# Attention chunk states from two running products, four pairs transposed on chip, and the whole instruction order in a table

## The chip, the cores and the metric

The kernel runs on one core of one Trainium2 chip. The metric is the device time of one execution in microseconds (us), lower is better. Engines: PE (matrix multiply), DVE (VectorE), ACT (ScalarE), POOL (GpSimd), and SP, whose queue issues every DMA.

## The reference, cut to what matters

A linear attention with a per-channel decay `w` is followed by two gated layers on the 3072 tokens.

```python
B, H, S, D = 4, 8, 768, 48
for t in range(S):                         # state: (B, H, D, D)
    cur = einsum('bhd,bhe->bhde', u[None] * k[:, :, t], v[:, :, t])
    y[:, :, t] = einsum('bhd,bhde->bhe', r[:, :, t], state + cur)
    state = w[:, :, t][..., None] * state + einsum('bhd,bhe->bhde', k[:, :, t], v[:, :, t])
x = y.transpose(0, 2, 1, 3).reshape(3072, 384)
x = ((x @ w_a) * (x @ w_b)) @ w_out                  # 384 -> 1536 -> 384
out = square(maximum(x @ w_in, 0)) @ w_out2          # 384 -> 2048 -> 384
```

## The kernel before

**Attention.** The sequence is cut into chunks of 64 tokens. Two chunks make a pair, and there are 24 pairs (6 for each of the 4 batches). All 8 heads of a pair are worked on together, with the even chunk on partitions 64 to 111 (`EV`) and the odd one on 0 to 47 (`OD`). For each pair, DVE forms the running product of the decays with one scan (`at_scan`, L307, into `ef`) and its reciprocals in four pieces of 128 columns (`at_recip`, L312). `k` times the reciprocal (`at_kr`, L316) and `r` times the product (`at_rr1` or `at_rr`) make all decays inside a chunk a product of two factors. `at_u1`, `at_u2` and `at_diag` form the diagonal term r·u·k from a second, untransposed copy of r and k (`nat`, 384 KB a pair). On PE a pair is four groups: A (scores, L361 and L362), B (transposes of k, L372), C (what each chunk adds to the state, L384 and L386) and D (outputs, L405 and L406). DVE merges the scores under a mask (L367, A2), and carries the state through both chunks with four operations (`at_C2`, L393 to L397). ACT copies D's result out of PSUM in two halves; SP stores it to `xd` in DRAM.

**Layers.** Weights arrive as 64-bit words, and each unit of layer weights is decoded by seven operations on ACT, DVE and POOL (L248, L252, L257 and L266 are those on DVE; L266 is the last). Every product is taken as three passes over high and low parts, so a block of n tokens costs 27 matmuls of n columns for each of the 12 units of the first layer (L431 to L433 up, L461 to L463 down) and 18 for each of the 16 of the second. The blocks of the first layer are `BLOCKS1 = [384, 256, 384] + [512] * 4`, so the first block needs pairs 0 to 2. Its tokens come back from `xd` (`plan_x`), are split into `xh` on ACT and `xl` on DVE (L631) or POOL, and the first matmul of the layer waits for the last `xl`.

**Order.** `Plan` orders all operations on all engines by costs and due times (`KNOB`), and every engine works through its own list in that order. For the first part of the program a table, `LEAD`, overrides the planner: each entry is an operation's number and, where it can run on several engines, a letter for the engine.

Of the kernel before, what the change touches and what calls it, by code (L numbers as in the profile page):

```python
# [27 lines left out]
BLOCKS1 = [384, 256, 384] + [512] * 4  # L28
# [6 lines left out]
EN = HE + HC  # L35
WS = 256.0

KNOB = dict(RC=42.49, START=12.8, LEAD=15.73, DEC=3.63, XO=5.02, X2=16.11, D2=32.51, LW=5.1, LT=30.17, LV=9.31,
            LV2=-10.85, LN=16.64, scan=3.63, rec=-5.73, kr=108.97, rr=-10.63, u1=0.34, u2=-43.62, dg=-15.47,
            gd=-190.45, UB=-979.54, A=9.27, B=166.95, C=-4.55, D=102.51, T2=4.07, EARLY=3.1, WAIT=0, U0=-2.33,  # L40
            DA=3.18, OB=26.94, P0=-44.22, P1=-28.21, P2=-11.48, P3=-11.11, P4=13.86, P5=83.07, P6=89.76, P7=90.37)
ENG = dict(kr=("POOL",), da=("DVE", "POOL"), dl=("DVE", "POOL"), rr=("POOL", "DVE"), u2=("DVE",), xs=("DVE",), d2=("ACT",),
           b2=("ACT",), gl=("POOL",), gh=("ACT",), dg=("POOL",), u1=("POOL",), ds=("DVE",))
ENG0 = dict(ENG, kr=("DVE",), rr=("POOL",))
NP0 = 7
ALONE = 8
SAFE = 2.0 ** 90
# [128 lines left out]
def fused_kernel(ctx, tc, tpk, natpk, vpk, v2pk, upk, cst, w1pk, w2pk, out):  # L176
# [126 lines left out]
    def inv(p):  # L303
        return EF[p][:, HE:]
# [644 lines left out]
```

## Time and profile before

| | |
|---|---|
| runs | 984.85, 987.32, 987.61 us, median 987.32 |
| the profiled execution | 984.9 us |
| its span, first to last instruction | 983.1 us |
| PE busy | 935.7 us, 95% of the span |
| DVE, ACT, POOL busy | 505.2, 387.6, 384.0 us |

The span is what the trace covers; the execution's own time is 1.8 us longer. A busy share of the whole says little here: the program starts with some 60 us of attention on four pairs and of decoding, in which PE is mostly idle, and then runs matmuls to its end. So the stretches are read one by one.

### The profile page before, as it was taken

The numbers are of one execution on the slowest core, as the hardware profiler recorded it, in microseconds if no ns is written. First come the engines' busy times: TensorE is split into PE (matmuls) and PEld (weight loads), VectorE is DVE, ScalarE is ACT, GpSimd is POOL, SyncE is SP. The second block draws the span as 40 slices with busy tenths as digits, with TensorE's granted clock in tenths as the row PEclk, the third lists the DMA queues.
The fourth block names the chain that finished last, engine by engine and source line by source line (L and its number), as shares of the span: only waits on it lengthen the run. The fifth ranks groups of instructions, "written<-read, shape, count | busy, mean of one in ns | idle before, by whom it ended". The sixth has DMA issues, their size and how long they took to land.

```text
span 983.1 us, 15022 instructions
## 1 busy us (share of the span) xinstructions
PE 935.7 (95%) x5982; PEld 799.3 (81%) x5982; DVE 505.2 (51%) x652; ACT 387.6 (39%) x600; POOL 384.0 (39%) x295
## 2 busy tenths in 40 slices
PE   2469999999999999999999999999999999999997
PEld 2459989999888888888888888888888888888885
DVE  7999999999755455532211789621121211211211
ACT  2677743343223332323322676433333333333332
POOL 5533177820165556543122444333333333333332
PEclk9569999999999999999999999999999999999999
DMA  8997336555022432220103562010000100100001
GB/s 224 258 288 225 112 89 178 145 162 157 25 82 81 139 108 69 85 65 29 48 33 113 193 212 95 0 65 1 33 33 1 53 11 1 65 1 1 33 0 36
DMA packets 58031, 87.17 MB, mean 89 GB/s; under 512 B 23904, under 2 KB 34912, under 8 KB 57952
## 3 DMA queue, kind: packets, MB, share of 16 engines
q1 hardware_dynamic: 57952, 86.12, 28.8%
q8 instruction: 49, 0.80, 0.3%
q14 instruction: 30, 0.25, 0.1%
HBM read 71.95 MB, written 14.16 MB: 88 GB/s over the span
## 4 chain that ended last, share of the span: by engine, by line
PE 84%; DVE 6%; DMA 6%; issue 1%; SPq 1%; ACT 0%; DVEq 0%; ACTq 0%
PE pa L431 15%; PE pa L432 15%; PE pa L433 15%; PE acc L461 11%; PE acc L462 11%; PE acc L463 11%; DMA raw<-in_w1pk_dram 2%; PE sc L361 2%; PE yp L405 2%; DMA rk<-in_tpk_dram 2%; DMA xd<-ys 1%; DVE ef L312 1%; DVE z L252 1%; PE ds L386 1%; DVE w L266 1%
## 5 line engine op out<-in xcount | busy, mean ns | idle before, releaser
L454 POOL TENSOR_TENSOR gl<-a,gh 128x512 fp32r<-128x512 f32 (+2 forms) x158 | 209.2, 1324 | 468.2 <-ACT gh L230 465.5
L431 PE MATMUL pa<-xh,w 128*128 128x512 f32 (+2 forms) x792 | 296.0, 374 | 1.4 <-ACT a L438 0.6
L432 PE MATMUL pa<-xl,w 128*128 128x512 f32 (+2 forms) x792 | 293.6, 371 | 0.6 <-DVE xl L631 0.6
L433 PE MATMUL pa<-xh,w 128*128 128x512 f32 (+2 forms) x792 | 293.6, 371 | 0.0
L438 ACT ACTIVATE a<-pa 128x512 f32<-128x512 f32 (+2 forms) x180 | 102.1, 567 | 289.5 <-PE pa L433 228.2
L461 PE MATMUL acc<-gh,w 128*128 128x512 f32 (+2 forms) x540 | 205.5, 381 | 0.0
L463 PE MATMUL acc<-gl,w 128*128 128x512 f32 (+2 forms) x540 | 202.5, 375 | 0.0
L462 PE MATMUL acc<-gh,w 128*128 128x512 f32 (+2 forms) x540 | 202.4, 375 | 0.0
L442 DVE TENSOR_TENSOR a<-a 128x512 f32<-128x512 f32 x96 | 68.3, 712 | 254.3 <-ACT a L438 254.3
L230 ACT ACTIVATE gh<-a 128x512 fp32r<-128x512 f32 (+2 forms) x174 | 105.2, 606 | 182.6 <-DVE a L442 125.4
L431 PEld LDWEIGHTS pa<-xh,w 128*128 128x128 f32 x792 | 149.5, 189 | 26.4 <-DVE a L442 1.6
L432 PEld LDWEIGHTS pa<-xl,w 128*128 128x128 f32 x792 | 149.5, 189 | 23.3 <-issue 0.9
L433 PEld LDWEIGHTS pa<-xh,w 128*128 128x128 f32 x792 | 149.4, 189 | 23.0
L461 PEld LDWEIGHTS acc<-gh,w 128*128 128x128 f32 x540 | 101.4, 188 | 17.8 <-DVE o L234 0.4
L463 PEld LDWEIGHTS acc<-gl,w 128*128 128x128 f32 x540 | 101.5, 188 | 17.0
L462 PEld LDWEIGHTS acc<-gh,w 128*128 128x128 f32 x540 | 101.5, 188 | 16.2
L442 DVE TENSOR_TENSOR a<-a,pa 128x512 f32<-128x512 f32 (+2 forms) x84 | 50.5, 602 | 109.2 <-PE pa L433 101.7
L312 DVE RECIPROCAL ef<-ef 112x128 f32<-112x128 f32 x96 | 84.4, 919 | 0.3
L367 DVE COPY_PREDICATED ar<-csb,sc 64x512 f32<-64x512 int32 x48 | 35.3, 735 | 32.7 <-PE sc L362 30.8
L307 DVE TENSOR_TENSOR_SCAN ef<-ef,floor 112x520 f32<-112x520 f32 x24 | 34.9, 1456 | 19.6 <-DMA ef<-in_tpk_dram 19.6
L405 PE MATMUL yp<-ar,vs 112*48 112x64 f32 x384 | 30.3, 237 | 12.3 <-ACT ar L230 8.2
L405 PEld LDWEIGHTS yp<-ar,vs 112*48 112x48 f32 x384 | 25.9, 135 | 19.0 <-ACT ar L230 8.7
(71 smaller groups left out, 893.8 us busy)
## 6 DMA issues: line engine op xcount, KB each, us to landing
raw<-in_w1pk_dram SPq DMA_DIRECT2D x36, 384.0 KB, 6.8
raw<-in_w2pk_dram SPq DMA_DIRECT2D x32, 384.0 KB, 4.1
rk<-in_tpk_dram SPq DMA_DIRECT2D x24, 448.0 KB, 4.7
nat<-in_natpk_dram SPq DMA_DIRECT2D x24, 384.0 KB, 3.3
ef<-in_tpk_dram SPq DMA_DIRECT2D x24, 227.5 KB, 3.6
vs<-in_vpk_dram SPq DMA_DIRECT2D x48, 96.0 KB, 3.0
v<-in_v2pk_dram SPq DMA_DIRECT2D x48, 96.0 KB, 3.4
xd<-ys SPq DMA_DIRECT2D x48, 96.0 KB, 2.4
```

The costliest lines, as they stand in the source:

```text
L230: nc.scalar.activation(out=out, in_=in_, func=ACTF.Copy, **({} if scale is None else {"scale": scale}))
L312: nc.vector.reciprocal(out=hv(inv(p), C)[:, h0:h0 + 2], in_=hv(ext(p), C + 1)[:, h0:h0 + 2, 1:])
L405: nc.tensor.matmul(out=P[OD, cs], lhsT=vs[0:112, 0, es], rhs=ar[0:112, 0, cs], start=True, stop=True)
L431: nc.tensor.matmul(out=out, lhsT=blk(wh, k), rhs=h, start=(k == 0), stop=False)
L432: nc.tensor.matmul(out=out, lhsT=blk(wh, k), rhs=l, start=False, stop=False)
L433: nc.tensor.matmul(out=out, lhsT=blk(wl, k), rhs=h, start=False, stop=(k == KD - 1))
L438: nc.scalar.activation(out=a[:, 0:n], in_=P[:, 0:n], func=func, scale=scale)
L442: eng(e).tensor_tensor(out=a[:, 0:n], in0=a[:, 0:n], in1=b[:, 0:n], op=ALU.mult)
L454: eng(e).tensor_tensor(out=gl[:, 0:n], in0=g[:, 0:n], in1=gh[:, 0:n], op=ALU.subtract)
L461: nc.tensor.matmul(out=acc[d][:, c0:c0 + m], lhsT=blk(wh, d), rhs=gh[:, 0:m], start=first, stop=False)
L462: nc.tensor.matmul(out=o, lhsT=blk(wl, d), rhs=gh[:, 0:n], start=False, stop=False)
L463: nc.tensor.matmul(out=o, lhsT=blk(wh, d), rhs=gl[:, 0:n], start=False, stop=last)
```

## The change

1. **Two running products, no reciprocals of them.** A first scan goes through the decays from the end (`at_bwd`, operands with a negative step) and gives the product from each token to the end of its chunk. One reciprocal of 8 columns and a second scan (`at_fwd`) give the product from the start, already divided by the chunk's whole product. `k` is multiplied by the first (`at_kb`, 63 of 64 columns), `r` by the second. The four reciprocals of 128 columns go.
2. **State operations one by one.** `at_C2` becomes four operations that the order can place apart, with the factor now taken from the first product.
3. **Diagonal term of pairs 0 to 5 from PE.** `at_rk` multiplies r and k in the transposed layout, 16 one-column matmuls in B sum them with u into PSUM, and `at_diag1` on DVE takes that PSUM column as an operand. For these pairs the `nat` load (384 KB), `at_u1` and `at_u2` go. The guard on ACT becomes two operations.
4. **Pairs 0 to 3 transposed on chip.** D gives [tokens, channels], ACT copies it, three transposes (`at_T`) turn it, and ACT and DVE split it straight out of PSUM. The store to DRAM and the load from it go for these pairs. For the others D's even half is widened to 64 rows, and ACT copies both halves in one operation.
5. **Blocks** `[512, 256, 256] + [512] * 4`: the first block needs pairs 0 to 3.
6. **Order.** `LEAD` now covers the whole program, `KNOB` has new values; POOL also does `rk`, and some `gl`, decode and `rr` operations change engine.

```diff
-BLOCKS1 = [384, 256, 384] + [512] * 4
+BLOCKS1 = [512, 256, 256] + [512] * 4
-EN = HE + HC
+EN = 2 * HE
-NP0 = 7
+NP0 = 6
+NPN = 4
 LEAD = """
-    0 4 34 5V 2573 31 6V 8V 7V 35 1 16P 36V 62 2572 17V 47P 9V 11P 2 37V 32 10P 696 48P 14A 12A 39V 38V 18V 24 40V 66
...
+    0 3 2 27 4V 1 5V 2540 31V 54 665 7V 28 6V 32V 8V 19 675 58V 666 9A 20A 11A 34P 169 16 10V 13A 12V 33P 676 15 21V
...
+    def at_bwd(p):
+        nc.vector.tensor_tensor_scan(out=rev(bwd(p)), data0=rev(ext(p)), data1=rev(floor[:, :]), initial=1.0, op0=ALU.mult,
+                                     op1=ALU.max)
+    def at_fwd(p):
+        nc.vector.reciprocal(out=hv(FG, C + 1)[:, :, 0:1], in_=hv(bwd(p), C + 1)[:, :, 1:2])
+        nc.vector.tensor_tensor_scan(out=ext(p), data0=ext(p), data1=FG, initial=0.0, op0=ALU.mult, op1=ALU.max)
+    def at_kb(p, e="DVE"):
+        kh = hv(RK[p][:, TK:], C)[:, :, 0:C - 1]
+        eng(e).tensor_tensor(out=kh, in0=kh, in1=hv(bwd(p), C + 1)[:, :, 2:], op=ALU.mult)
+    def at_rk(p, e="DVE"):
+        t = RK[p]
+        eng(e).tensor_tensor(out=AR[p % 2][0:112, 1, :], in0=t[:, TR:TK], in1=t[:, TK:], op=ALU.mult)
+    def at_diag1(p, c):
+        rows = slice(c * C, c * C + C)
+        nc.vector.tensor_tensor(out=hv(AR[p % 2][rows, c, :], C),
+                                in0=ident[rows, rows].rearrange("p (o t) -> p o t", o=1).to_broadcast([C, H, C]),
+                                in1=PS[p, "B"][rows, 448:448 + H].rearrange("p (h o) -> p h o", o=1).to_broadcast([C, H, C]),
+                                op=ALU.mult)
     def at_B(p):
...
+        if p < NP0:
+            rk = AR[p % 2][:, 1, :]
+            for h in range(H):
+                cs, o = slice(h * C, (h + 1) * C), slice(448 + h, 449 + h)
+                nc.tensor.matmul(out=P[0:C, o], lhsT=rk[EV, cs], rhs=ucols[EV, h:h + 1], start=True, stop=True)
+                nc.tensor.matmul(out=P[C:128, o], lhsT=rk[OD, cs], rhs=ucols[OD, h:h + 1], start=True, stop=True)
     def at_D(p):
         ar, vs = AR[p % 2], VS[p % 2]
+        if p < NPN:
+            P = PS[p, "D"] = ps_at.tile([128, DM], F32, tag="at", name="yn")
+            for h in range(H):
+                cs, es = slice(h * C, (h + 1) * C), slice(h * D, (h + 1) * D)
+                nc.tensor.matmul(out=P[0:C, es], lhsT=ar[0:112, 0, cs], rhs=vs[0:112, 0, es], start=True, stop=True)
+                nc.tensor.matmul(out=P[C:128, es], lhsT=ar[:, 1, cs], rhs=vs[:, 1, es], start=True, stop=True)
+            return
...
+    def at_T(p):
+        P = PS[p, "T"] = ps_at.tile([128, KD, 128], F32, tag="at", name="yt")
+        y = YS.pop(p)
+        for k in range(KD):
+            nc.tensor.transpose(P[:, k, :], y[:, k * 128:(k + 1) * 128], ident)
+    def plan_t(key, p, i, c0, last):
...
+        def hi(e):
+            if i == 0:
+                xs[key] = new_x()
+            copy(e, xs[key][0][:, :, cols], PS[p, "T"])
+        def lo(e):
+            x = xs[key]
+            nc.vector.tensor_tensor(out=x[1][:, :, cols], in0=PS.pop((p, "T")), in1=x[0][:, :, cols], op=ALU.subtract)
```

How the instructions move is seen at three places. In these rows an operation stands with its line, what it writes and reads, and its shape; a scan is listed as SCALAR_TENSOR_TENSOR.

The first place is DVE at the start of the program, from the first scan to the diagonal of pair 0. Before:

```order
L307 SCALAR_TENSOR_TENSOR ef<-ef,floor 112x520
L312 RECIPROCAL ef<-ef 112x128 x3
L307 SCALAR_TENSOR_TENSOR ef<-ef,floor 112x520
L337 TENSOR_TENSOR nat<-nat,u_sb 128x384
L312 RECIPROCAL ef<-ef 112x128 x4
L341 TENSOR_REDUCE dg<-nat 128x8
L312 RECIPROCAL ef<-ef 112x128
L350 TENSOR_TENSOR ar_88<-csb,dg 64x512
```

And in the changed kernel:

```order
L396 SCALAR_TENSOR_TENSOR ef<-ef,floor 112x520
L401 RECIPROCAL fg<-ef 112x8
L402 SCALAR_TENSOR_TENSOR ef<-ef,fg 112x520
L396 SCALAR_TENSOR_TENSOR ef<-ef,floor 112x520
L429 TENSOR_TENSOR ar_90<-rk 112x512
L407 TENSOR_TENSOR rk<-rk,ef 112x8x63
L401 RECIPROCAL fg<-ef 112x8
L402 SCALAR_TENSOR_TENSOR ef<-ef,fg 112x520
L420 TENSOR_TENSOR rk<-rk,ef 112x512
L396 SCALAR_TENSOR_TENSOR ef<-ef,floor 112x520
L450 TENSOR_TENSOR ar_90<-csb,kt 64x512 x2
```

Eight reciprocals have given way to four further scans, and r·k, k and r of pair 0 are multiplied on DVE rather than on POOL.

The second place is DVE around the last `xl` of the first block, the operation that lets the first layer begin. Before, pairs 0 and 1 have their `xl` here and pair 2's is on POOL:

```order
L367 COPY_PREDICATED ar_89<-csb,sc 64x512 x2
L350 TENSOR_TENSOR ar_88<-csb,dg 64x512
L248 TENSOR_SCALAR raw_393<-raw_393 128x1152
L393 TENSOR_TENSOR ds<-ds,vs_91 48x384
L394 TENSOR_TENSOR vs_91<-ds,ef 48x384
L396 TENSOR_TENSOR ds<-ds,vs_91 48x384
L397 TENSOR_TENSOR vs_90<-ds,ef 48x384
L252 SCALAR_TENSOR_TENSOR z<-z,raw_393 128x1152
L631 TENSOR_TENSOR xl<-xl,xh 128x3x128
L257 ISA z<-raw_393,z 128x2304
L266 TENSOR_TENSOR w_509<-z,w_509 128x1152
```

In the changed kernel, where pairs 1 to 3 end:

```order
L479 COPY_PREDICATED ar_91<-csb,sc 64x512 x2
L513 TENSOR_TENSOR ds<-ds,vs_93 48x384
L515 TENSOR_TENSOR vs_93<-ds,ef 48x384
L446 TENSOR_REDUCE dg<-nat 128x8
L517 TENSOR_TENSOR ds<-ds,vs_93 48x384
L519 TENSOR_TENSOR vs_92<-ds,ef 48x384
L779 TENSOR_TENSOR xl<-yt,xh 128x3x128
L407 TENSOR_TENSOR rk<-rk,ef 112x8x63
L401 RECIPROCAL fg<-ef 112x8
L402 SCALAR_TENSOR_TENSOR ef<-ef,fg 112x520
L779 TENSOR_TENSOR xl<-yt,xh 128x3x128 x2
L396 SCALAR_TENSOR_TENSOR ef<-ef,floor 112x520
```

Before, DVE's part of three units and the sign of a fourth (L248) stand ahead of the last `xl`; in the changed kernel only the first two steps (sign and shift) of two units do, and the tail of pair 3 is followed at once by its `xl`.

The third place is SP's queue up to the third and last load of the first weight unit. Before:

```order
L281 DMA ef<-in_tpk_dram 112x520
L743 DMA csb<-in_cst_dram 128x192
L298 DMA v_93<-in_v2pk_dram 64x384 x2
L285 DMA rk<-in_tpk_dram 112x1024
L219 DMA raw_152<-in_w1pk_dram 128x768
L289 DMA nat<-in_natpk_dram 128x768
L298 DMA v_94<-in_v2pk_dram 64x384 x2
L219 DMA raw_152<-in_w1pk_dram 128x768
L289 DMA nat<-in_natpk_dram 128x768
L292 DMA vs_90<-in_vpk_dram 64x384
L293 DMA vs_90<-in_vpk_dram 64x384
L219 DMA raw_152<-in_w1pk_dram 128x768
```

And in the changed kernel:

```order
L364 DMA ef<-in_tpk_dram 112x520
L368 DMA rk<-in_tpk_dram 112x1024
L921 DMA csb<-in_cst_dram 128x264
L364 DMA ef<-in_tpk_dram 112x520
L302 DMA raw_142<-in_w1pk_dram 128x768
L368 DMA rk<-in_tpk_dram 112x1024
L302 DMA raw_172<-in_w1pk_dram 128x768
L302 DMA raw_142<-in_w1pk_dram 128x768
L372 DMA nat<-in_natpk_dram 128x768
L302 DMA raw_172<-in_w1pk_dram 128x768
L302 DMA raw_142<-in_w1pk_dram 128x768
```

Of the `nat` loads only one is left ahead of the first unit, and two loads of the second unit have come in between.

## Rows read from the trace of the kernel before

**Rows 1.** The page: busy us (share of the span) and instructions of each engine.

```profile
PE 935.7 (95%) x5982; PEld 799.3 (81%) x5982; DVE 505.2 (51%) x652; ACT 387.6 (39%) x600; POOL 384.0 (39%) x295
```

**Rows 2.** Windows: busy us (instructions) of each engine, granted clock, DMA share, GB/s.

```profile
core 0: us, PE busy (x) PEld busy (x) DVE busy (x) ACT busy (x) POOL busy (x), PEclk, DMA share, GB/s
0.00:20.00 20.00, 4.62 (x55) 3.91 (x56) 15.36 (x20) 4.44 (x7) 10.62 (x18) 1.00 0.85 223
20.00:40.00 20.00, 10.63 (x168) 8.97 (x166) 19.44 (x29) 8.90 (x13) 13.30 (x11) 0.66 0.97 253
40.00:60.00 20.00, 6.87 (x86) 5.71 (x86) 19.68 (x25) 15.88 (x20) 9.36 (x6) 0.51 0.81 233
60.00:80.00 20.00, 18.67 (x152) 17.67 (x153) 19.24 (x25) 13.61 (x18) 6.83 (x3) 0.81 1.04 346
140.00:200.00 60.00, 60.00 (x714) 57.47 (x715) 57.78 (x87) 22.97 (x48) 48.01 (x39) 1.00 0.54 149
600.00:700.00 100.00, 100.00 (x443) 82.81 (x442) 40.38 (x43) 40.45 (x61) 33.07 (x25) 1.00 0.05 16
```

**Rows 3.** PE's waits from 66 to 976 us: the longest of two.

```profile
PE pa L431 <- ACT a L438: 0.6, 1, 0.6
```

**Rows 4.** Timeline, PE: first matmuls of the first layer, and the last one.

```profile
62.63 0.69 PE L431 MATMUL pa<-xh,w 128*128 128x384 f32 x1
63.89 0.66 PE L432 MATMUL pa<-xl,w 128*128 128x384 f32 x1 [0.57 <-DVE xl L631]
...
975.75 0.39 PE L463 MATMUL acc<-gl,w 128*128 128x512 f32 x1
```

**Rows 5.** Groups of DVE's instructions by shape, 0 to 63.8 us.

```profile
L312 DVE RECIPROCAL ef<-ef 112x128 f32<-112x128 f32 x18 | 15.5, 914 | 0.1
L307 DVE TENSOR_TENSOR_SCAN ef<-ef,floor 112x520 f32<-112x520 f32 x5 | 6.2, 1232 | 3.4 <-DMA ef<-in_tpk_dram 3.4
L367 DVE COPY_PREDICATED ar<-csb,sc 64x512 f32<-64x512 int32 x8 | 5.8, 728 | 0.3
L350 DVE TENSOR_TENSOR ar<-csb,dg 64x512 f32<-64x512 f32 x5 | 5.0, 1004 | 0.0
L394 DVE TENSOR_TENSOR vs<-ds,ef 48x384 f32<-48x384 f32 x4 | 2.2, 560 | 0.1
L316 DVE TENSOR_TENSOR rk<-rk,ef 112x512 f32<-112x512 f32 x1 | 0.7, 679 | 0.0
```

**Rows 6.** The same groups, 63.8 to 140 us.

```profile
L266 DVE TENSOR_TENSOR w<-z,w 128x1152 fp32r<-128x1152 f32 x9 | 12.2, 1351 | 0.0
L252 DVE SCALAR_TENSOR_TENSOR z<-z,raw 128x1152 int32<-128x1152 int32 x8 | 10.8, 1355 | 0.0
L257 DVE CUSTOM_DVE_ANT_0 z<-raw,z 128x2304 uint16<-128x2304 uint16 x7 | 9.5, 1355 | 0.1
L248 DVE TENSOR_SCALAR raw<-raw 128x1152 int32<-128x1152 int32 x8 | 6.1, 758 | 0.1
L350 DVE TENSOR_TENSOR ar<-csb,dg 64x512 f32<-64x512 f32 x1 | 0.6, 618 | 0.0
```

**Rows 7.** The same groups, whole span and 140 to 480 us (the last two rows).

```profile
L442 DVE TENSOR_TENSOR a<-a,pa 128x512 f32<-128x512 f32 x48 | 32.8, 684 | 105.4 <-PE pa L433 99.8 <-ACT z L230 5.4
...
L312 DVE RECIPROCAL ef<-ef 112x128 f32<-112x128 f32 x66 | 58.3, 920 | 0.2
L307 DVE TENSOR_TENSOR_SCAN ef<-ef,floor 112x520 f32<-112x520 f32 x16 | 24.4, 1522 | 16.2 <-DMA ef<-in_tpk_dram 16.2
```

**Rows 8.** Timelines: DVE's first scan; ACT's first step on a weight unit.

```profile
3.72 1.24 DVE L307 TENSOR_TENSOR_SCAN ef<-ef,floor 112x520 f32<-112x520 f32 x1 [2.15 <-DMA ef<-in_tpk_dram]
25.48 1.26 ACT L230 ACTIVATE z<-raw 128x1152 f32<-128x1152 f32 x1 [3.69 <-DMA raw<-in_w1pk_dram]
```

**Rows 9.** Windows of PE's group A, pairs 0 and 1: length, PE busy (records).

```profile
17.84:19.74 1.90, 1.90 (x32) 1.78 (x32) 0.00 (x0) 1.00 0.94 238
21.18:22.12 0.94, 0.94 (x32) 0.94 (x32) 0.00 (x0) 1.00 0.95 353
```

More of the change, by code (lines that the diff above doesn't have):

```diff
@@ L447, in split_hi @@
         if fill:
[L448 removed]
+            nc.vector.memset(gh[:, n:NB].bitcast(F32), 0.0)
         copy(e, gh[:, 0:n], g[:, 0:n])
@@ L511, in fused_kernel, with late @@
     K = KNOB
+    def late(on):
+        return {**KNOB, **{k[1:]: v for k, v in KNOB.items() if k[0] == "z"}} if on else KNOB
     tau = [K["START"]]
@@ L533, in plan_pair @@
         add("LV", {"DMA": 2 * t_dma(96)}, K["LV"], lambda e: at_load_v(p), [("D", p - 2)], lat=DMA_LAT)
-        add("LN", {"DMA": t_dma(384)}, K["LN"], lambda e: at_load_n(p), [("LN", p - 1)], acq=[("nat", p)], lat=DMA_LAT)
-        add("scan", {"DVE": 1.27}, K["scan"], lambda e: at_scan(p), [("LT", p)], port=True)
-        for k in range(4):
-            add(("rec", k), {"DVE": 0.87}, K["rec"] - k, lambda e, k=k: at_recip(p, k), [("scan", p)])
-        add("kr", both(0, HC, *E0["kr"]), K["kr"], lambda e: at_kr(p, e), [("LRK", p), *((("rec", k), p) for k in range(4))],
-            port=True)
@@ L549, in plan_pair @@
-        for k in range(2):
-            add(("u1", k), both(0, DM, *E0["u1"]), K["u1"], lambda e, k=k: at_u1(p, k, e),
-                [("LN", p), (("u1", k - 1), p), "usb"], port=True)
-        add("u2", {"DVE": 0.55}, K["u2"], lambda e: at_u2(p, e), [(("u1", 1), p), ("u2", p - 1)], acq=[("dg", p)],
-            rel=[("nat", p)])
-        add("gd", {"ACT": 1.27}, K["gd"], lambda e: at_guard(p),
-            [(("rr", 0), p), (("rr", 1), p), ("A", p), ("B", p), ("C2", p)], rel=[("rk", p), ("ef", p)])
@@ L556, in plan_pair @@
-        alone = p < ALONE
-        depA, acqA = [("kr", p), *([("rr1", p)] if p < NP0 else [(("rr", 0), p), (("rr", 1), p)]), ("A", p - 1)], [("at", (p, "A"))]
+        add("sb", {"DVE": 1.27}, K["scan"], lambda e: at_bwd(p), [("LT", p)], port=True)
+        add("sf", {"DVE": 1.4}, K["sf"], lambda e: at_fwd(p), [("sb", p)], port=True)
+        U, alone, last = p < NP0, p < ALONE, p % PPB == PPB - 1
+        add("kb", both(0, HC, *E0["kr"]), K["kr"], lambda e: at_kb(p, e), [("LRK", p), ("sb", p), ("rk", p)], port=True)
@@ L589, in plan_pair @@
+        add("D2", both(0, DM if p < NPN else HC, *ENG["d2"]), K["D"], lambda e: at_D2(p, e), [("D", p)], acq=[("ky", (p, "y"))],
+            rel=[("at", (p, "D"))])
+        if p < NPN:
+            add("T", {"PE": 0.35 * cold}, K["D"], lambda e: at_T(p), [("D2", p)], acq=[("at", (p, "T"))], rel=[("ky", (p, "y"))])
+        for c in range(0 if p < NPN else 2):
+            add(("ST", c), {"DMA": 0.6}, K["D"], lambda e, c=c: at_store(p, c), [("D2", p), (("ST", c - 1), p)],
                 rel=[("ky", (p, "y"))] if c else [], lat=DMA_LAT)
@@ L618, in plan_x @@
             first, last = i == 0, i == len(pieces) - 1
+            if load in range(NPN):
+                plan_t(key, load, i, c0, last)
+                continue
             k, cols = (*key, i), slice(c0, c0 + n)
```

363 lines of the change are left out of this document (243 added, 120 removed).

## The prediction

> **What bounds the kernel now.** I read the page first, then the windows, then PE's waits, then DVE's groups in the window that the waits point to. PE is busy for 935.7 of 983.1 us [rows 1], so about 47 us at most could come from PE's idle time, and the windows say where it is: PE works 4.62, 10.63 and 6.87 us in the first three stretches of 20 us, and nearly all the time afterwards [rows 2]. The first matmul of the first layer stands at 62.63 us, but the second waits until 63.89, for DVE's last `xl` of the first block; the last layer matmul starts at 975.75 [rows 4]. Between 66 and 976 us PE has two waits, the longest of 0.6 us [rows 3]. So the program is two pieces: a start of 63.9 us, and 912 us of matmuls with a 7 us end. Whoever shortens the start by x, and leaves PE fed, takes x off the time.
>
> The start is DVE's. It is busy for 19.44 and 19.68 of 20 us in its second and third stretch [rows 2]; PE idles, mostly at the lower of its two clock levels, 1.2 GHz (granted 0.66 and 0.51 on average), ACT and POOL are half idle. DVE's groups up to 63.8 us show what fills it: the largest is the 18 reciprocals, 15.5 us, against 6.2 us for the scans [rows 5]. The only waits DVE has there are 3.4 us for the loads of `ef`. The queues are busy too (DMA share 0.97 from 20 to 40 us, at 253 GB/s), so a faster DVE must not outrun its loads.
>
> **The start, part by part.** I add up DVE's list in the changed kernel up to the last `xl` of the first block, by its order and the durations of before.
>
> - Scans: 10 (both products of pairs 0 to 3, and of pair 4) at 1.23 us [rows 5] = 12.3 us. The operands with a negative step are in no row. Lower bound 1.23, no reason to be quicker; upper bound the reciprocal's pace, 914 ns for 128 columns, 3.7 us for 520. I take 1.23, the nearest row: same operation, same width.
> - Reciprocals: 18 before (15.5 us) become 5 of 8 columns. By columns 0.06 us each, at most 0.91 [rows 5]; I take 0.1, 0.5 us in all. Here is the gain: 15.5 us go, and 5 additional scans, 6.2 us, come.
> - Products with r and k on DVE, 5 at 0.68 [rows 5]: 3.4 us. The others are on POOL.
> - Diagonal from PSUM, 8 operations. The same shape from SBUF took 1.00 us on average in this stretch and 0.62 undisturbed [rows 5, 6]; I take 0.62 (5.0 us) and keep 8.0 for the range.
> - A2, 8 at 0.73: 5.8 us. State operations, 15 at 0.56: 8.4 us [rows 5]; being apart costs nothing by itself, and lets DVE do other work while PE catches up. Four `xl` from PSUM, priced like these, 2.2 us.
> - Decoding: 2 signs and 2 shifts, 0.76 and 1.36 us [rows 6]: 4.2 us. Before, DVE's work on three units stood here. This part is moved, not saved; it comes back below.
> - `nat` product, one reduction, one memset, near 0.5 us each: 1.5 us.
>
> The sum is 43.3 us. DVE's first scan starts at 3.72 us [rows 8]; without gaps the last `xl` would end at 47. Gaps: the first sign needs ACT's first step on the first unit, and that its third load. Before, that step began at 25.48, after a wait on the load [rows 8]. The new queue puts 4.4 MB up to that load (from the shapes); at 223 GB/s [rows 2] and a start near 2.3 us it lands at 22, and ACT is done at 23.5. DVE would be there at 19.6, so it stands about 3.9 us; the waits on the first `rk` and on PE's first groups lie inside this. The shift then waits for ACT's second step, 0.5 us. The loads of pairs 3 and 4 (7.1 and 9.5 MB) land near 33 and 43 us, ahead of use, because 2.4 MB of `nat` is gone. I add 0.7 us for the end D, ACT, transpose, ACT, `xl` of pair 3, most of which lies beside a product, a scan and the chain of states. **Last `xl` at 52.4 us instead of 63.9: 11.5 us less.** The store to DRAM and the load back go for four pairs; they cost DMA time and latency that this new end does not have.
>
> PE's new work: 16 one-column matmuls per pair, 32 records. Group A has 32 records and took 1.90 us at the start, 0.94 later [rows 9]; the columns would make it far less, so 0.2 to 1.9 us. Four pairs lie in the idle start, pair 4's also; pair 5's lies in the matmul piece: +0.6 us. Twelve transposes lie in the start.
>
> **The first block.** 10 of 12 units have to be decoded while PE runs it: DVE's list from there to the last `L349` has 10 decodes at 0.76 + 3 x 1.35 = 4.8 us [rows 6], 48.2; 10 products of 512 columns at 0.68 [rows 7], 6.8; 7 low parts on DVE at the same price, 4.8; 6 scans, 7.4; 4 A2 and 7 state operations, 6.8; 4 diagonals, 2.5; five small ones, 2.5. Sum 79 us, so the last unit is ready at 131.4, and PE, with one step of 27 matmuls left, is through the block at 138.2. PE's own work from 52.4: a matmul of 512 columns comes every 0.226 us (443 in 100 us, [rows 2]), so 12 x 27 x 0.226 = 73.3; three pairs at an estimated 3.1 us (A takes 0.94 [rows 9], C and D about as much, B a third), and 1 us for the first matmuls at the lower clock: 135.9. DVE is late by 2.3 us. To that **I add 2.2 us for POOL**, which makes the stall 4.5 us. At the start POOL was busy for 33 of 60 us and the scans still took 1.23; from 140 us on, with POOL busy 48 of 60 us, they took 1.52 on average, while the reciprocals stayed at 0.91 and 0.92 [rows 2, 5, 7]. So an operation that reads two operands from SBUF is held up by POOL, a reciprocal isn't, and the change swaps the one for the other. The Trainium skill (SBUF — State Buffer, "SBUF: two separate sides") says that VectorE with two SBUF inputs and GpSimd take the shared port pair in turn, each for a whole instruction; the trace agrees with its direction, and by the rule taken strictly the sum would be the second rival's.
>
> Later stages: PE waits for nothing there, the same 20 pairs and the same columns are left, and DVE is 51% busy over the span. ACT's saved copies and guard changes lie beside PE: nothing. If the new order put a late operand before PE, that would be a loss; I see the same sequence D, C, A in a batch as before.
>
> **Sum.** 983.1 - 11.5 + 0.6 + 4.5 = 976.7 us of span, 978.5 with the 1.8 us around it, against 984.9 for the profiled execution. That one is at the low end of the three runs (median 987.32); I put the new median 1 us above its like, at **979.5**.
>
> **Rivals.**
> 1. *Nothing is stalled.* POOL and DVE stay out of each other's way and the first block runs at PE's pace: 983.1 - 11.5 + 0.6 = 972.2, 974 to 975 for the run; with `xl` free of the first gap, 968. For it: the order was written out for both engines together. Against: 79 us of DVE work in 78 of PE's leave no slack. Chance 0.22.
> 2. *POOL and DVE take turns.* DVE's operations with two SBUF operands, from the first scan to the last decode: 16 scans, 12 shifts, 20 other decode steps, 7 low parts, 6 products, some 72 us. Stretched as the scans were after 140 us (1.52 / 1.23, 24%) they cost 17 us, 15 more than I allow: 991.7, 993.5 for the run. In proportion to POOL's load in this stretch, a third of the time rather than 80%, it is 7, and the run is 983 to 985. For it: the scans of [rows 7]. Against: scans at 1.23 beside a half-busy POOL [rows 2, 5]. Chance 0.12, most of it near the lower price.
> 3. *The reversed scan is slow, and the kernel is slower than before.* Eight of them lie on DVE's path up to the last decode. At the reciprocal's pace each costs 2.5 us more, 19.8 us: 996.5, 998 for the run. It decides the sign above 6.4 + 3 us, 1.2 us a scan, that is from 2.4 us on. Against: a scan works one column after another in either direction. Chance 0.06.
> 4. *The start's gain is given back*: loads or the order leave DVE idle for 6 us more between 10 and 130 us (the queue's share was 0.81 to 0.97 before): 982 to 985 for the run, near no change. Chance 0.08.
>
> **How the numbers follow.** My forecast has 0.52. A measurement of this kernel tells 0.3% from no change, 3 us: faster means below 984.4. The forecast, rival 1 and parts of 2 and 4 lie there: 0.80. Rivals 2 and 4 give most of the 0.11 within, rival 3 and the upper part of 2 the 0.09 above. The range goes from rival 1's low end, 968, to 988, which takes in the lower price of rival 2, rival 4 and the 3 us of the diagonals.
>
> **What would show it.** Right: the last `xl` at 50 to 55 us; scans in both directions near 1.23; no reciprocal of 128 columns; DVE over 95% busy to 130 us; PE waits of some 4 to 6 us in the first block, mostly on `w` or `gl`, and next to none later. Wrong: scans over 2 us, an `xl` after 58, or PE waits after 140 us, which this sum has at nothing.

## The result and the profile after

The changed kernel takes **975.25 us** (median of four runs, 972.72 to 977.49) against 986.28 us for the kernel before, run beside it. The ratio is 0.9893, 95% interval 0.9879 to 0.9907: faster by 1.1%. The forecast was 979.5.

The profiled execution took 975.67 us. PE's records cut both profiled executions into the same three pieces: up to the second matmul of the first layer, from there to the last layer matmul, and the rest of the span.

| us | before | after | difference | forecast |
|---|---|---|---|---|
| start | 63.89 | 50.64 | -13.25 | -11.5 |
| matmul piece | 911.86 | 915.69 | +3.83 | +5.1 |
| end | 7.37 | 7.47 | +0.10 | 0 |
| span | 983.1 | 973.8 | -9.3 | -6.4 |

The timelines of PE show the borders, as [rows 4] did before:

```profile
49.90 0.49 PE L565 MATMUL pa<-xh,w 128*128 128x512 f32 x1
50.64 0.50 PE L566 MATMUL pa<-xl,w 128*128 128x512 f32 x1 [0.25 <-DVE xl L779]
...
966.33 0.39 PE L597 MATMUL acc<-gl,w 128*128 128x512 f32 x1
```

The page's line of busy times answers to [rows 1]; DVE has only 7 us less over the span, POOL 36 us less:

```profile
PE 948.3 (97%) x6186; PEld 797.8 (82%) x6186; DVE 498.1 (51%) x627; ACT 380.7 (39%) x627; POOL 348.4 (36%) x259
```

The windows answer to [rows 2] (same columns):

```profile
0.00:20.00 20.00, 8.58 (x116) 7.60 (x118) 14.95 (x25) 4.73 (x9) 7.10 (x15) 1.00 0.82 241
20.00:40.00 20.00, 18.55 (x265) 16.51 (x265) 19.06 (x27) 14.36 (x24) 11.78 (x7) 1.00 0.88 254
40.00:60.00 20.00, 17.29 (x181) 13.91 (x180) 19.58 (x29) 12.38 (x19) 11.77 (x7) 0.91 0.88 257
60.00:80.00 20.00, 18.40 (x193) 14.09 (x189) 19.67 (x23) 13.70 (x20) 8.35 (x5) 1.00 0.91 294
80.00:100.00 20.00, 18.69 (x151) 14.04 (x150) 19.88 (x21) 14.76 (x20) 6.07 (x3) 1.00 0.25 68
100.00:140.00 40.00, 40.00 (x208) 33.15 (x207) 38.38 (x45) 22.66 (x29) 6.42 (x5) 1.00 0.35 104
```

DVE is the full engine of the start still. PE is busier there, and its granted clock stays near the upper level (1.00 and 0.91, where [rows 2] have 0.66 and 0.51); the 0.91 is 0.50 from 51 to 54 us, just behind the start, and 1.00 before. PE's waits from 66 to 967 us, answering to [rows 3], come to 2.2 us, all for DVE (total, times, longest):

```profile
PE pa L565 <- DVE a L576: 2.0, 2, 1.1
PE pa L567 <- DVE w L349: 0.2, 1, 0.2
```

DVE's groups by shape up to 50.6 us answer to [rows 5]. The scans go both ways at one price, 1.24 us; the first row's mean is raised by a sixth scan, begun at 50.51, that took 1.60:

```profile
L396 DVE TENSOR_TENSOR_SCAN ef<-ef,floor 112x520 f32<-112x520 f32 x6 | 7.8, 1295 | 2.5 <-DMA ef<-in_tpk_dram 2.4
L402 DVE TENSOR_TENSOR_SCAN ef<-ef,fg 112x520 f32<-112x520 f32 x5 | 6.2, 1242 | 0.2
L450 DVE TENSOR_TENSOR ar<-csb,kt 64x512 f32<-64x512 f32 x8 | 5.5, 685 | 0.9 <-ACT kn L313 0.6
L401 DVE RECIPROCAL fg<-ef 112x8 f32<-112x8 f32 x5 | 1.0, 202 | 0.1
```

Its groups from 53 to 140 us answer to [rows 6]. The shift (L335), the last decode step (L349) and the forward scan (L402) take longer than there, the other two of these rows don't:

```profile
L335 DVE SCALAR_TENSOR_TENSOR z<-z,raw 128x1152 int32<-128x1152 int32 x10 | 15.6, 1560 | 0.0
L349 DVE TENSOR_TENSOR w<-z,w 128x1152 fp32r<-128x1152 f32 x10 | 14.4, 1444 | 0.0
L340 DVE CUSTOM_DVE_ANT_0 z<-raw,z 128x2304 uint16<-128x2304 uint16 x10 | 13.5, 1346 | 0.0
L331 DVE TENSOR_SCALAR raw<-raw 128x1152 int32<-128x1152 int32 x10 | 7.5, 749 | 0.1
L402 DVE TENSOR_TENSOR_SCAN ef<-ef,fg 112x520 f32<-112x520 f32 x3 | 4.6, 1524 | 0.1
```

### The profile page after: what moved, and what is told of

Same layout as the page of the kernel before. It is cut to its first block, busy times and chain, and to the rows that moved or that the text cites. A ratio compares the mean times of both kernels' runs of the same rounds, so it can differ in the third digit from the quotient of the medians.

```text
span 973.8 us, 15176 instructions
## 1 busy us (share of the span) xinstructions
PE 948.3 (97%) x6186; PEld 797.8 (82%) x6186; DVE 498.1 (51%) x627; ACT 380.7 (39%) x627; POOL 348.4 (36%) x259
## 4 chain that ended last, share of the span: by engine, by line
PE 91%; DVE 5%; issue 1%; DMA 1%; SPq 1%; ACT 0%; DVEq 0%; ACTq 0%
PE pa L565 16%; PE pa L567 16%; PE pa L566 16%; PE acc L595 12%; PE acc L597 12%; PE acc L596 12%; PE sc L473 2%; PE yp L535 1%; PE yp L536 1%; PE kt L484 1%; PE ds L502 1%; DVE z L335 1%; DVE ar L479 1%; PE ds L504 1%; DMA rk<-in_tpk_dram 1%
## 5 line engine op out<-in xcount | busy, mean ns | idle before, releaser
L588 POOL TENSOR_TENSOR gl<-a,gh 128x512 fp32r<-128x512 f32 (+1 forms) x147 | 206.1, 1402 | 463.6 <-ACT gh L313 456.9
L565 PE MATMUL pa<-xh,w 128*128 128x512 f32 (+1 forms) x792 | 295.6, 373 | 2.2 <-DVE a L576 2.0
L567 PE MATMUL pa<-xh,w 128*128 128x512 f32 (+1 forms) x792 | 293.9, 371 | 0.2 <-DVE w L349 0.2
L566 PE MATMUL pa<-xl,w 128*128 128x512 f32 (+1 forms) x792 | 293.6, 371 | 0.2 <-DVE xl L779 0.2
L595 PE MATMUL acc<-gh,w 128*128 128x512 f32 (+1 forms) x540 | 205.7, 381 | 0.0
L572 ACT ACTIVATE a<-pa 128x512 f32<-128x512 f32 (+1 forms) x180 | 102.4, 569 | 256.5 <-PE pa L567 224.2
L596 PE MATMUL acc<-gh,w 128*128 128x512 f32 (+1 forms) x540 | 202.6, 375 | 0.0
L597 PE MATMUL acc<-gl,w 128*128 128x512 f32 (+1 forms) x540 | 202.6, 375 | 0.0
L313 ACT ACTIVATE gh<-a 128x512 fp32r<-128x512 f32 (+1 forms) x180 | 108.2, 602 | 229.9 <-DVE a L576 195.9
L576 DVE TENSOR_TENSOR a<-a,pa 128x512 f32<-128x512 f32 (+1 forms) x84 | 51.2, 610 | 151.4 <-PE pa L567 150.5
L335 DVE SCALAR_TENSOR_TENSOR z<-z,raw 128x1152 int32<-128x1152 int32 (+1 forms) x23 | 35.7, 1552 | 0.1
L402 DVE TENSOR_TENSOR_SCAN ef<-ef,fg 112x520 f32<-112x520 f32 x24 | 34.3, 1428 | 0.8
```

The costliest lines, as they stand in the source:

```text
L313: nc.scalar.activation(out=out, in_=in_, func=ACTF.Copy, **({} if scale is None else {"scale": scale}))
L335: nc.vector.scalar_tensor_tensor(out=z, in0=z, scalar=3, in1=words(u, n)[:, :, 1], op0=ALU.logical_shift_left, op1=ALU.bitwise_or)
L565: nc.tensor.matmul(out=out, lhsT=blk(wh, k), rhs=h, start=(k == 0), stop=False)
L566: nc.tensor.matmul(out=out, lhsT=blk(wh, k), rhs=l, start=False, stop=False)
L567: nc.tensor.matmul(out=out, lhsT=blk(wl, k), rhs=h, start=False, stop=(k == KD - 1))
L572: nc.scalar.activation(out=a[:, 0:n], in_=P[:, 0:n], func=func, scale=scale)
```

## The experiments

Each run is the changed kernel with one edit. Ratios are to the kernel before on the same chip; the three pieces come from each run's one profile.

| run | start | matmul piece | end | median us | ratio (95%) |
|---|---|---|---|---|---|
| changed kernel | 50.64 | 915.69 | 7.47 | 975.25 | 0.9893 (0.9879 to 0.9907) |
| 18 reciprocals, start | 65.11 | 915.65 | 7.30 | 990.0 | 1.0044 (1.0027 to 1.0061) |
| `nat` loads | 54.49 | 914.28 | 9.15 | 979.1 | 0.9931 (0.9915 to 0.9948) |
| through DRAM | 60.98 | 911.42 | 9.78 | 984.09 | 0.9982 (0.9972 to 0.9991) |
| states together | 52.44 | 922.40 | 7.55 | 985.71 | 0.9999 (0.999 to 1.0009) |
| no POOL | 50.10 | 913.07 | 7.45 | 973.49 | 0.9878 (0.9862 to 0.9895) |
| signs on ACT | 52.15 | 911.68 | 7.78 | 973.91 | 0.9881 (0.9864 to 0.9897) |
| shorter list | 50.12 | 914.43 | 7.50 | 974.0 | 0.9878 (0.9861 to 0.9894) |
| signs, other form | 51.63 | 912.21 | 7.37 | 973.36 | 0.9873 (0.9856 to 0.9891) |
| shorter list, other form | 50.82 | 914.31 | 7.50 | 973.45 | 0.987 (0.9852 to 0.9887) |
| 64 reciprocals, late | 50.81 | 946.83 | 7.49 | 1005.37 | 1.0196 (1.0179 to 1.0213) |
| the same, work to POOL | 50.71 | 943.06 | 7.63 | 1003.21 | 1.0168 (1.0146 to 1.019) |
| the same, spread | 50.21 | 934.74 | 7.41 | 994.11 | 1.0085 (1.0068 to 1.0101) |

### What sets the start: reciprocals, loads, transposes

The start's reciprocals come back:

```diff
+        for i in range(4 if p < 4 else 2 if p == 4 else 0):
+            nc.vector.reciprocal(out=scr, in_=bwd(p)[:, i * 128:(i + 1) * 128])
```

> The 18 reciprocals of 128 columns that stood in the start before are issued again on DVE, beside the change, into a scratch tile that nothing reads (four each for pairs 0 to 3, two for pair 4). Theory (DVE's list sets when the start ends): 18 x 0.914 = 16.5 us more on DVE, less what fills its 2 us of waits; the last xl of the first block goes from 50.6 to 65 to 67 us, and the time from 975.3 to 989 to 992. Rival (the loads or PE bound the start now, DVE has slack): the last xl moves by less than 5 us, time 975 to 980.

The theory holds: the start is 14.5 us longer, the matmul piece is the same to 0.04 us, the time 990.0. DVE spent 16.9 us on them, so some 2.4 us of its earlier waits are gone:

```profile
L404 DVE RECIPROCAL scr<-ef 112x128 f32<-112x128 f32 x18 | 16.9, 940 | 0.4
```

The loads that went with the diagonal's new form:

```diff
+        if p < NP0:
+            nx = wp.tile([128, 2 * DM], F32, tag=f"w{(11, 9, 7, 10, 6, 11)[p]}", name="nx")
+            nc.sync.dma_start(out=nx, in_=natpk[p])
```

> The nat loads of pairs 0 to 5 are issued again behind their rk loads, into memory that nothing reads: 2.36 MB, 9.4 us of the queues' time at 250 GB/s, nothing on an engine. Theory (DVE sets the start, its loads come ahead of use): 0 to 3 us, time 975 to 978. Rival (the queues set the start, so the loads saved are the gain): 7 to 10 us, time 982 to 985.

Between the two: start 3.85 us later, time 979.1. The queues don't set the start, but nor are loads free. In this one profile the last `xl` ends 2.4 us later (53.01), and PE, granted 0.50 from 48 to 56 us where the change has 1.00 up to 51, adds the rest. So the loads cost at most 0.4 us for each us of queue time.

Pairs 0 to 3 through DRAM, with `LEAD` rewritten for the added and removed operations:

```diff
-NPN = 4
+NPN = 0
```

> Pairs 0 to 3 go through DRAM again (NPN = 0): two stores and one load a pair in place of three transposes, the split moved to where the load should have landed, with other DVE work put ahead of the last one. All else as in the change. Theory (the end of the start is what the transposes shorten): the first layer's second matmul goes from 50.6 to 53 to 57 us, time 978 to 981. Rival (the store and the load hide beside DVE's list): under 1.5 us, time 974 to 977.

The direction is the theory's, the size twice as large: the start is 10.3 us longer, of which the matmul piece gives 4.3 back. DVE runs ahead on the first block's decoding meanwhile: it has done 7.8 us of it when the first layer begins, against 4.2 in the change. Each load from DRAM waits in SP's queue for its store, and holds up the loads behind it. This kernel's waits, SP's from 40 to 60 us and ACT's from 20 to 64 (total, times, longest):

```profile
SPq L865 <- DMA xd<-ys: 5.2, 2, 2.6
...
ACT xh L310 <- DMA xl<-xd: 6.2, 3, 4.3
```

PE's timeline shows what ACT's last such wait costs:

```profile
60.35 0.79 PE L562 MATMUL pa<-xh,w 128*128 128x512 f32 x1 [5.44 <-ACT xh L310]
```

How much of the 10.3 us another order of these operations would save is open. So is the split of the change's 13.25 us: the undone parts add up to more. The start also took in a fourth pair, and it gave up decoding, and no run undid either. DVE's signs and shifts of 128x1152 in the start, before (up to 63.7 us) and after (up to 50.6):

```profile
L252 DVE SCALAR_TENSOR_TENSOR z<-z,raw 128x1152 int32<-128x1152 int32 x4 | 5.4, 1354 | 0.1
L248 DVE TENSOR_SCALAR raw<-raw 128x1152 int32<-128x1152 int32 x4 | 3.8, 938 | 0.0
```

```profile
L335 DVE SCALAR_TENSOR_TENSOR z<-z,raw 128x1152 int32<-128x1152 int32 x2 | 2.7, 1342 | 0.0
L331 DVE TENSOR_SCALAR raw<-raw 128x1152 int32<-128x1152 int32 x2 | 1.5, 761 | 0.1
```

Before, four signs and four shifts stood ahead of the last `xl` (the fourth unit's shift too), with one further step (L257) and one last step (L266) of 1.35 us each: 11.9 us of decoding, against 4.2 now. So 7.7 us of DVE's shorter list is work moved behind the start, where PE has matmuls to run; the reciprocals, less the added scans, are 8.3 us of it.

### The state operations

In `LEAD` the four of a pair stand together where the last one stood, and D and the guard's second step (44, 41) go behind them where they need them. For pair 1:

```diff
-    40A 672P 48V 73 49V 895V 50V 41A 82 74A 85V 678A 62P 64V 44 51V
+    40A 672P 73 895V 82 74A 85V 678A 62P 64V 48V 49V 44 41A 50V 51V
```

> The four state operations of each pair stand together again on DVE, at the place of the last of them, and the groups D and guards that need them behind them. The instructions are the same. Theory (being apart lets DVE do other work while PE catches up): the waits that the pieces hid come back, at the start above all, 1 to 3 us, time 976 to 979. Rival (the order of the four among the others doesn't matter): 974 to 976.

A miss: 985.7 us, all of the change's gain lost. The start is only 1.8 us longer; 6.7 us are in the matmul piece, most of them between 140 and 260 us, where PE idles for 5.5 us and in the changed kernel not at all. There DVE waits for loads of `rk`, for which it waits nowhere in this stretch in the changed kernel:

```profile
DVE ar L410 <- DMA rk<-in_tpk_dram: 5.7, 2, 2.9
DVE gl L584 <- ACT gh L309: 3.5, 3, 1.8
```

SP's queue shows why. The second and the last state operation read `ef`, and an `ef` load waits there until its buffer is free, with the `rk` loads behind it in the queue. Such waits from 165 to 201 us, in this run and in the change:

```profile
SPq L360 <- DVE vs L511: 20.1, 2, 10.6
```

```profile
SPq L364 <- DVE vs L515: 3.9, 2, 3.4
```

Both lines name the second state operation. The `rk` loads that DVE waits for here were issued 2 and 4 us after these two waits. The guard reads `ef` too, and the run moves its second step as well, but no wait for it stands in this stretch of SP's queue (in the change one of 3.4 us does). What the guards' places would cost alone isn't shown.

### What the first block costs

```diff
+GONE = {("rr", 4), ("rr", 5), ("rk", 5), (("u1", 1), 7), ("kb", 6), (("rr", 0), 6), (("rr", 1), 6), (("dg", 1), 6)}
...
+            if ops[i][0] not in GONE:
                 ops[i][3](e)
```

> Left out: eight POOL operations that fall into the first block (r products of pairs 4, 5 and 6, r times k of pair 5, k of pair 6, one product of nat and one diagonal), some 12 us of POOL between 50 and 95 us; nothing of DVE's list is left out. Theory (POOL holds up DVE's operations with two SBUF operands, which makes DVE late in the first block): the shifts, scans and decode steps there fall back to 1.23 and 1.35 us, PE's gaps between 54 and 100 us (some 6 us of the 8.1 above the columns' time) shrink by 2 to 4 us, time 971 to 973. Rival (DVE is late by its own sum, POOL costs nothing): 974.5 to 976.

In the mechanism the theory is right. From 53 to 140 us, shift and last decode step are back at 1.35 us (columns as above); the matmul piece is 2.6 us shorter, while the median, 973.49, lies just above the range named, with an interval that overlaps the change's:

```profile
L337 DVE SCALAR_TENSOR_TENSOR z<-z,raw 128x1152 int32<-128x1152 int32 x10 | 13.5, 1351 | 0.0
L351 DVE TENSOR_TENSOR w<-z,w 128x1152 fp32r<-128x1152 f32 x9 | 12.1, 1348 | 0.0
```

The stretch of DVE's ten shifts and ten last steps by POOL is thus 10 x (1.560 - 1.351) + 10 x (1.444 - 1.348) = 3.1 us, where the prediction allowed 2.2. The forward scans, still 1.52 us on average here, aren't in it: one of three takes 2.09 us beside a `gl` of POOL that this run keeps. With it the hold is 4.0 us. The means come from a few meetings: of the change's ten shifts three are long (1.57, 2.25 and 2.33 us), of its ten last steps one (2.35).

Two tries to shorten DVE's list: the sign steps on ACT by their letter in `LEAD`, and the same with unit 1's and with pair 4's second scan (113), two steps of pair 6's diagonal (175, 176) and what hangs on them behind the last `xl` (901):

```diff
-690V 700V 710V 720V 730V 740V 750V 760V 770V 780V
+690A 700A 710A 720A 730A 740A 750A 760A 770A 780A
...
-    113V 127 900A 94A 899V 116P 715 901V
+    127 900A 94A 899V 715 901V 113V 175V 176V 116P
```

> The sign step of weight units 2 to 11 on ACT in place of DVE, at the same places of the order: 10 x 0.75 us less on DVE in the first block, 10 x 1.2 us more on ACT, whose share there is 60 to 70%. Theory (DVE's list bounds the first block): PE's gaps shrink by 2 to 4 us, time 971 to 973. Rival (the chain through ACT is what PE waits for, and gets longer): 975 to 979.

> Signs of units 1 to 11 on ACT, and three DVE operations that the first block's xl don't need (second scan of pair 4, second product and sum of pair 6's diagonal) moved behind the last xl, with the nat load of pair 7 and the product it feeds moved later. Theory (the last xl ends when DVE's list does): the list up to it is 3.3 us shorter, of which the chain through PE and ACT at the end takes some back, the second matmul goes from 50.6 to 47.5 to 48.5 us; with the signs off DVE the first block doesn't give it back: time 968 to 971. Rival (the chain through PE and ACT sets the end of the start, or the first block gives it back): 973 to 977.

ACT's step doesn't leave the sign word that DVE's does, and the other form (scale 0, bias minus zero) doesn't either; why is open. These four runs stand for the time alone.

> As the run with the signs of units 2 to 11 on ACT, with a form of the step there (scale 0, bias minus zero) that keeps the sign. Theory (DVE's list bounds the first block): the matmul piece is 3 to 4 us shorter than the change's 915.7, time 971 to 974. Rival (the start, or ACT's longer chain, gives it back): 975 to 977.

> The same for units 1 to 11, with the three DVE operations and pair 7's nat load behind the last xl. Theory (both the start and the first block are DVE's): start 0.5 to 2 us and matmul piece 1 to 4 us shorter, time 970 to 973. Rival (the chain through PE and ACT after the last state operation sets the start's end, and the moved operations delay the first block): as without the move, or 1 us more, 972 to 975.

With the signs off DVE, the matmul piece is 4.0 and 3.5 us shorter, as the theory has it. But the start of the same two profiles was 1.5 and 1.0 us longer with nothing in the lists ahead of it changed. That is PE's: DVE's last `xl` ends at 50.66 and 50.40 there, as in the change, while pair 4's one-column matmuls, which PE runs just ahead of the layer, took 1.80 us instead of 1.03. In the second profile its granted clock was 0.50 there, in the change 1.00 (48 to 51 us, columns as in [rows 2], change first; the first profile's record reads 1.00 at the slower pace):

```profile
48.00:51.00 3.00, 2.50 (x40) 1.90 (x40) 2.97 (x6) 2.97 (x7) 1.18 (x1) 1.00 0.95 335
```

```profile
48.00:51.00 3.00, 3.00 (x39) 2.72 (x37) 2.96 (x6) 2.82 (x7) 1.19 (x1) 0.50 1.00 314
```

The last layer matmul starts 2.5 us earlier than in the change in both. The medians, 973.9 and 973.4, can't be told from the change's: their intervals overlap. The moved operations gave no shorter start than 50.1 us. In the run named shorter list the last state operation ends 1.4 us earlier than in the change, and DVE then waits 1.03 us for ACT's `xh`, the end of the chain from D through ACT and the transposes:

```profile
45.12 0.55 DVE L515 TENSOR_TENSOR vs<-ds,ef 48x384 f32<-48x384 f32 x1
45.70 0.56 DVE L775 TENSOR_TENSOR xl<-yt,xh 128x384 fp32r<-128x384 f32 x1
46.18 0.67 DVE L403 TENSOR_TENSOR rk<-rk,ef 112x504 f32<-112x504 f32 x1
47.88 0.56 DVE L775 TENSOR_TENSOR xl<-yt,xh 128x384 fp32r<-128x384 f32 x1 [1.03 <-ACT xh L309]
```

Its last `xl` ends at 49.15, 1.4 us ahead of the change's, but the second matmul starts only 0.5 us earlier, at 50.12. PE is the last there: from 46.4 us on it shows no wait through the transposes, pair 4's group B and the first layer matmul. So in the change's order DVE's list, this chain and PE's own list end within about 1 us of each other.

### Is DVE free later?

```diff
+        for i in range(4 if p >= 8 else 0):
+            nc.vector.reciprocal(out=scr, in_=bwd(p)[:, i * 128:(i + 1) * 128])
```

> The same reciprocals, four each for pairs 8 to 23, 64 x 0.92 = 59 us of DVE work, all behind the start and the first block. Theory (only the start and the first block lie on DVE's path): no change, 974 to 977. Rival (DVE's total counts, or its later waits reach PE): 980 or more.

The theory fell: 1005.4 us. The kernel before carried reciprocals like these behind 140 us [rows 7], and PE waited for nothing. Two runs ask why it can't here.

> The 64 late reciprocals again, and 18 operations of blocks 1 and 2 (eleven low parts gl, five diagonals, two products with r) go from DVE to POOL, about as many as POOL had more of before: 10 us less on DVE between 140 and 300 us, some 19 us more on POOL, which is busy for 46 of 160 us there. Theory (the changed order has spent the time that the reciprocals left on DVE on work of POOL, so DVE has no slack up to 250 us): the 30 us that the reciprocals cost fall by 5 to 12, time 993 to 1000. Rival (it is the reciprocals' place between the two scans of a pair that delays what follows, not DVE's total): 1003 or more.

The rival's range: 1003.2 us. Handing 18 operations to POOL helps by 2 us only, which is not clear of the noise: the two intervals overlap.

```diff
+    def extra(p, i):
+        if p >= 8:
+            nc.vector.reciprocal(out=scr, in_=floor[:, i * 128:(i + 1) * 128])
...
+        extra(p, 0)
```

The four calls stand behind a pair's two scans, behind A2 and behind its last state operation.

> The same 64 late reciprocals, but one at a time: one behind each of a pair's two scans, one behind A2, one behind its last state operation, instead of four in a row between the scans. Total DVE work as in the run with 64 late reciprocals. Theory (the four in a row, 3.7 us of DVE, are longer than the slack that PE's two product buffers give in a block of 256 columns; the total would fit): time 976 to 990. Rival (between 140 and 260 us DVE is full, so its total counts): 999 to 1008.

Neither range: 994.1 us. Spreading them saves 11 of the 30 us, 19 stay. The windows of 140 to 260 us (columns as in [rows 2]) of five kernels, in this order: before, change, 64 reciprocals in fours, the same with work to POOL, 64 spread:

```profile
140.00:260.00 120.00, 119.89 (x1235) 114.41 (x1236) 112.45 (x172) 43.54 (x86) 54.40 (x44) 1.00 0.49 138
```

```profile
140.00:260.00 120.00, 120.00 (x1348) 113.62 (x1347) 105.99 (x180) 42.31 (x107) 19.54 (x16) 1.00 0.50 134
```

```profile
140.00:260.00 120.00, 105.05 (x1151) 98.65 (x1150) 112.84 (x181) 35.28 (x93) 13.64 (x12) 0.96 0.42 114
```

```profile
140.00:260.00 120.00, 107.26 (x1177) 101.10 (x1176) 109.40 (x169) 36.99 (x94) 32.65 (x30) 0.96 0.41 114
```

```profile
140.00:260.00 120.00, 109.86 (x1249) 102.72 (x1247) 115.73 (x185) 36.47 (x93) 15.25 (x13) 0.97 0.43 119
```

Third number DVE, fifth POOL. The reciprocals that left this stretch have not made DVE idle: it is at 105.99 of 120 us after 112.45, and POOL has gone from 54.4 to 19.5. The order spent DVE's freed time on low parts, diagonals and products that POOL had. DVE has 14 us to spare here; the spread run puts 27 reciprocals of 0.94 us, 25 us, into its window. PE idles for 15.0 us of its window with the reciprocals in fours, for 10.1 with them spread, and most of these waits are for DVE's results (`a`, `gl`, `o`). A full DVE isn't all of it: with work handed to POOL DVE has 10.6 us to spare, more than in the spread run, and PE still idles for 12.7. So the place of four in a row between a pair's two scans costs some 11 us by itself; what part of the other 19 is DVE's sum isn't settled.

## Why the prediction held, point by point

1. **The start is DVE's.** Right, and shown by the 18 reciprocals: 14.5 us of start for 16.9 us of DVE. The forecast last `xl` was 52.4 us, the measured one 50.59. (The prediction's own terms, 47.0 and waits of 3.9, 0.5 and 0.7, give 52.1; 0.3 us has no term.) DVE's list came out at 44.3 us against a sum of 43.3: the small reciprocals took 0.20 each, not 0.1 (+0.5), the diagonals 0.685, not 0.62 (+0.5); scans, A2, states and decoding as summed. The **mis-sized term is the gaps**: some 5 us forecast, 2.6 measured. The largest of them, 3.9 us in front of the first sign, isn't there at all. ACT's first decode step began at 20.88, behind a copy and not behind the load, and DVE came to the sign only at 22.45, straight from a diagonal:

```profile
20.44 0.54 ACT L313 ACTIVATE kn<-kt 128x448 f32<-128x448 f32 x1 [4.18 <-PE kt L490]
20.88 1.25 ACT L313 ACTIVATE z<-raw 128x1152 f32<-128x1152 f32 x1
```

```profile
22.45 0.76 DVE L331 TENSOR_SCALAR raw<-raw 128x1152 int32<-128x1152 int32 x1
```

   The third load had landed at 18.5 us (8.8 us after its issue at 9.64), not at 22. The forecast's rate, 223 GB/s, is the mean of a window that begins at 0 [rows 2], and a start of 2.3 us was added to it once more. What DVE did wait for were loads of `ef` (0.9) and `rk` (0.7) and PE's and ACT's first groups (0.8). The longer list and the shorter gaps partly cancel, which is luck.
2. **One-column matmuls.** Pair 5's were put at 0.6 us in the matmul piece. They take 1.24 us there, from 64.70 to the next group at 65.95. All attention groups in the piece grew by 2.65 us, from 62.42 us (1648 records) to 65.07 (1676): 0.6 of it is PE's wait for the pair's own scores, which the prediction had not named, and 0.8 lies in groups C and D.
3. **The stall of the first block.** The last unit was ready at 131.15 us, 80.6 us after the last `xl`; the forecast was 79 us, and 2.2 for POOL. The stall was put at 4.5 us. (Its sum has a slip: 131.4 and a step of 27 x 0.226 us make 137.5, not 138.2, so its own terms make DVE late by 1.6 us, not 2.3.) PE did not wait for that unit at all: it came to it at 131.53, late itself. The layer matmuls' time above their columns' (0.0134 + n/2400 us, the planner's cost, 0.227 for 512, as [rows 2] have it) grew by 1.23 us over the piece (12.93 to 14.16). 8.1 us of the 14.16 lie ahead of 100 us: 1.7 in the first nine matmuls, of which seven took 0.2 us too long (granted clock 0.50 from 51 to 54 us), 2.0 waiting for products, 1.0 for a `v` load that the prediction had not named, 0.2 for an earlier unit's last step (81.16 to 83.51, held by POOL), and the rest in pieces of some 0.1 us. These two waits stand beside those shown above (50.7 to 140 us):

```profile
PE ds L502 <- DMA v<-in_v2pk_dram: 1.0, 1, 1.0
PE kt L484 <- PE sc L474: 0.6, 1, 0.6
```

   So the sign that the prediction named, waits of 4 to 6 us mostly on `w` or `gl`, came as 3.7 us with 0.2 on `w` and none on `gl`. That DVE is what holds PE up here is right: with 7.5 us of signs off DVE the last layer matmul comes 2.5 us earlier. Together points 2 and 3 gave 3.83 us for the 5.1 summed.
4. **POOL's hold on DVE.** Right as a mechanism; the term is mis-sized, 3.1 us in place of 2.2 by the run without POOL, 4.0 with the scan that it leaves held. The second rival, turn-taking at 983 us and more, is wrong in its price and right in its mechanism. In the changed kernel a shift takes 2.25 us instead of 1.35; POOL's product, begun 0.14 us ahead of it, ends at 61.03, and the shift 1.2 us later (POOL's row first):

```profile
59.84 1.19 POOL L420 TENSOR_TENSOR rk<-rk,ef 112x512 f32<-112x512 f32 x1
...
59.98 2.25 DVE L335 SCALAR_TENSOR_TENSOR z<-z,raw 128x1152 int32<-128x1152 int32 x1
```

   In the run through DRAM a product of 0.68 us took 3.09 beside a decode step of POOL that had begun 0.08 us ahead and took 2.63:

```profile
48.86 2.63 POOL L346 TENSOR_TENSOR w<-z,w 128x1152 fp32r<-128x1152 f32 x1
...
48.94 3.09 DVE L404 TENSOR_TENSOR rk<-rk,ef 112x504 f32<-112x504 f32 x1
```

   That is the rule of the Trainium skill (SBUF — State Buffer, "SBUF: two separate sides"), that whichever starts first keeps the port pair for its whole instruction; these rows agree with it, one instruction at a time. The price stays small because POOL has little to do there: 20.8 of 80 us from 60 to 140.
5. **Later stages: nothing.** Right in the outcome, wrong in its reason. "DVE is 51% busy over the span" said nothing of 140 to 260 us, where it is at 88%, and 59 us more of DVE work cost 30 us. A forecast of a change that added work there would have failed.
6. **Time.** The span came out 2.9 us below the 976.7 summed, 1.75 of it in the start (point 1), 1.3 in points 2 and 3. The added 1 us for the median didn't show: the profiled execution took 975.67, the median is 975.25. The result lies nearer to rival 1 (974 to 975) than to the forecast, though not for its reason: the matmul piece did lose 3.8 us, and the start gained more. Rival 3 (slow reversed scans) is out at 1.24 us a scan, and rival 4 (gain given back) too. The range's low end, 968, is a span of rival 1; as a time it would be 970.

## What to carry to other kernels

A share of busy time over the whole span is no slack: ask in each stage whether an engine could take more work, and remember that a new order may have spent the time that a cheaper operation freed. A transfer through DRAM costs more than its store and load when its wait stands in a queue with other loads behind it. An operation's place also sets when its buffers come free, and through the queue when other loads start. A window's mean rate holds the window's idle beginning; don't add that beginning again. Undo one part at a time and don't expect the parts to add up: here they came to more than the whole.

## What was not expected of the hardware

- A scan whose three operands run backwards takes what a forward one takes: 1.24 us for 112 x 520.
- POOL is held up as DVE is. Its product with k takes 1.17 us at 34.84, and 2.17 beside a shift of DVE from 23.73 to 25.08:

```profile
23.95 2.17 POOL L407 TENSOR_TENSOR rk<-rk,ef 112x504 f32<-112x504 f32 x1 [6.23 <-DVE ar L429]
...
34.84 1.17 POOL L407 TENSOR_TENSOR rk<-rk,ef 112x504 f32<-112x504 f32 x1
```

- The hold is not confined to operations with two operands. The sign step, which reads one, takes 0.73 us in the changed kernel where nothing holds it, and 2.28 beside a step of POOL begun 1.05 us ahead of it (POOL's row first):

```profile
552.12 2.72 POOL L340 TENSOR_TENSOR z<-z,raw 128x1152 int32<-128x1152 int32 x1 [2.56 <-DVE z L335]
...
553.17 2.28 DVE L331 TENSOR_SCALAR raw<-raw 128x1152 int32<-128x1152 int32 x1 [0.46 <-ACT z L313]
```

- The same lists, up to the first layer's matmul, gave starts from 50.2 to 52.2 us in six profiles, and ends from 7.3 to 9.8 us with the same instructions behind the last matmul. The two longest starts are PE's slower pace in them, as shown above. A difference below 2 us between two profiles is weak evidence; the parts of the sums in points 1 to 3 are readings of one profile each.
